# Sliding window attention with a normalized MLP: output buffers of group 0, column halves of W1, and the places of period 1's steps changed

## The chip, the cores and the metric

The kernel runs on one core of one Trainium2 chip. The metric is the time of one execution on the device, in microseconds (us). Engines: PE is TensorE, DVE is VectorE, ACT is ScalarE, POOL is GpSimd, SP is SyncE, which here only issues DMAs.

## The reference

For 8 batches of 576 positions and 8 heads of 64:

```python
scores = q @ k.T / 8              # per batch and head
mask = (rel >= 0) & (rel < 64)    # rel = query position - key position
attn = softmax(where(mask, scores, -1e9))
x = (attn @ v) with the heads side by side          # 8 x 576 x 512
xn = (x - mean) / sqrt(var + 1e-6) * g_ln           # over the 512 columns
out = x + relu(xn @ w_ch1) @ w_ch2                  # 512 -> 2048 -> 512
```

All inputs and the output are float32. The kernel casts what PE reads to float16 (f16) and accumulates in float32.

## The kernel before, in words

**Groups and periods.** Group g (0 to 7) is the first 512 positions of batch g; group 8 collects the last 64 positions of all eight batches, as four "tails" of two batches each. Period g is the loop turn in which the MLP of group g runs on PE. The attention of group g + 1 is worked in between, and the loads and casts of batch g + 2 go on beside it. Periods 6 and 7 carry the tails.

**A list of units and slots.** `mlp_units` returns the MLP of a group as a list of closures. The loop at the end of the kernel emits unit i, then every step that `at(i, ...)` put into slot i. The program order of each engine is that order; nothing is rescheduled later, and each engine works its queue strictly in order. `bz(i, g, j)` puts three steps of block j into slots i, i + 1 and i + 2: `b_step` (the product of the softmax weights with V, called the PV step, then on DVE the reciprocal, the scaling and the mean and variance: together a normalization), `r_step` (two ACT instructions for the reciprocal root) and `z_step` (DVE: the normalized block in f16). `zt_step` transposes z on PE into PSUM, and ACT copies it to zT, which the first product reads.

**First product.** `l1_half` (L440) makes two 128 x 256 results in one bank, `l1` (L408) one 128 x 512 result; either is 0.86 to 0.87 us of PE, and ACT applies relu (L445, L412). Group 0 has 8 half units and 8 whole ones, group 1 has 16 half units, the others 16 whole ones. They use the two banks of pool `ps_mm`.

**Second product.** Group 0 multiplies plainly: `l2_two` (L455) for output blocks 0 and 1, `l2` (L420) for blocks 2 and 3, and `add_out` (L429) adds x on DVE into a single buffer `osb1`, of which there are two, and appends a store on POOL's queue. All other groups use Strassen's scheme with seven products of half width (`product`, L480, units 16 to 29). `presum` makes the half sums on DVE (L398), `t_weights` those of the weights (L386, once). `post` (L495) adds a product into a pair buffer `osb`; a product that accumulates into a bank which an addition still reads has to wait for that addition. Bank X lives in pool `ps_t`, which has two banks, so that while X is held, transposes share the other bank.

**Attention.** `s_mm` computes the scores of one block of 128 queries against their keys (L279) into the two banks of pool `ps_s`, then ACT applies exp (L289, L283). The mask is either two matmuls ahead of the scores, which write a large negative bias (`pe_mask=True`, L261), or a product with 0 and 1 on DVE behind exp (`s_mask`, L296).

**Q, K and V.** SP loads them (L78, L83, L90, L144), POOL casts them (`cast_q` L131, `cast_v` L150). Batches below `NPE` are transposed on PE (`t_main`, L221, eight 128 x 128 transposes into PSUM and one copy on ACT or DVE, L213 or L215); the others by DMA from SP's queue (`x_main`, L233 and L239). `vB` is V shifted by 64 rows: for batches 0 and 1 copied by ACT and DVE (`vB_cur`, `vB_prev`), afterwards by two DMAs of POOL (`make_vB`, L168). `pace` (L348) is a one-column POOL copy that makes POOL wait for a certain result.

**Weights.** W1 is loaded in eight pieces of 256 rows x 512 columns; pieces 2q and 2q + 1 make the column quarter q. `w1_cast` scales by g and casts: chunk c = 0 of quarters 0 and 1 on POOL (L195), c = 1 on ACT (L193); quarters 2 and 3 on DVE and ACT. W2 is loaded in eight chunks into the same four staging buffers and cast on POOL (`w2_cast`, L205): chunk i serves unit `l2_two(i)`, and chunk i + 4 is loaded once chunk i has been cast.

**Warming matmuls.** `keep_clock` issues matmuls whose result nobody reads, at the start, while PE would otherwise idle.

Of the kernel before, what the change touches and what calls it, by code (L numbers as in the profile page):

```python
# [18 lines left out]
def kernel(  # L19
# [15 lines left out]
    NGRP = B + 1  # L35
    NPE = 4
    NKC = DM // 128
# [81 lines left out]
    def cast_qk(b, half):  # L119
        for x in range(2):  # L120
            cast_q(b, x, half)
# [130 lines left out]

    def s_mm(g, j, pe_mask=False):
        sc = [ps_s.tile([128, NHP, 2, 64], FP32, tag="sc", name=f"sc_{g}_{j}_{par}") for par in range(2)]
        pt = p_pt.tile([128, 2, NHP, 2, 64], FP16, tag="pt", name=f"pt_{g}_{j}")
# [144 lines left out]
    def mlp_units(g, split=0, two=False):  # L400
# [12 lines left out]

        ch = {}

# [11 lines left out]
        def add_out(kb):  # L427
            o = p_blk.tile([128, DM], FP32, tag="osb1", name=f"osb_{g}_{kb}", bufs=2)
            nc.vector.scalar_tensor_tensor(  # L429
                out=o, in0=ch[kb], scalar=rss[(g, kb)][:, 0:1],  # L430
                in1=x_norm[(g, kb // 2)][:, kb % 2].rearrange("p h d -> p (h d)"), op0=ALU.mult, op1=ALU.add,
            )
            stores.append((cur[0], nc.gpsimd, out[g, 128 * kb:128 * kb + 128, :], o))
# [28 lines left out]
        lo, hi = slice(0, 256), slice(256, 512)  # L462
        xyz, oo = {}, {}

# [80 lines left out]
    nc.vector.tensor_scalar(out=mbias, in0=mask, scalar1=-1.0, scalar2=30000.0, op0=ALU.add, op1=ALU.mult)  # L545
    for b in range(2):
        alloc_qkT(b)
        alloc_v(b)
        init_vB(b)
    cast_qk(0, 0)  # L550
    cast_v(0, 0, 1)
# [6 lines left out]
    w1_cast(1, 0, nc.gpsimd, 256, 512)  # L558
    w1_cast(2, 0, nc.gpsimd)
    w1_cast(3, 0, nc.gpsimd)  # L560

    warm = ps_mm.tile([128, 512], FP32, tag="mm", name="warm")

    def keep_clock(n):
# [24 lines left out]
    keep_clock(1)  # L589
    t_main(0, 1, 1, 0)  # L590
    keep_clock(2)
    b_step(0, 1)
    z_step(0, 1)
    keep_clock(2)
    vB_prev(0, 2, 0)
    vB_cur(0, 3, 1)
    s_mm(0, 2, True)
    zt_step(0, 0)
    w1_cast(0, 1, nc.scalar)
    b_step(0, 2)  # L600
    z_step(0, 2)
    zt_step(0, 1)
    w1_cast(1, 1, nc.scalar)
# [10 lines left out]
    def rest_of_loads():  # L614
        for i in range(8):
# [11 lines left out]
    TAILS = {  # L627
        6: ((0, load_tail, 0), (3, cast_tail, 0), (7, x_tail, 0), (14, s_mm, 8, 0), (15, s_mask, 8, 0),
            (20, b_step, 8, 0), (26, zt_step, 8, 0),
            (9, load_tail, 1), (12, cast_tail, 1), (16, x_tail, 1), (20, load_tail, 2), (24, cast_tail, 2),  # L630
            (28, x_tail, 2)),
        7: ((0, s_mm, 8, 1), (1, s_mask, 8, 1), (6, b_step, 8, 1), (12, zt_step, 8, 1),
            (6, s_mm, 8, 2), (7, s_mask, 8, 2), (11, b_step, 8, 2), (17, zt_step, 8, 2),
            (0, load_tail, 3), (3, cast_tail, 3), (7, x_tail, 3), (14, s_mm, 8, 3), (15, s_mask, 8, 3),
            (20, b_step, 8, 3), (26, zt_step, 8, 3)),
    }
    for g in range(NGRP):
# [12 lines left out]
        if g == 0:  # L650
# [5 lines left out]
            at(1, zt_step, 0, 2)  # L656
            at(3, zt_step, 0, 3)
            for j in range(4):
# [19 lines left out]
            at(29, vB_cur, 1, 3, 0)  # L678
            at(29, s_mm, 1, 2, True)
            at(30, s_mm, 1, 3, True)  # L680
            at(30, load_v, 2, 0, 4)
            bz(31, 1, 2)
            at(21, cast_q, 2, 0, 0)
            at(22, lambda: pace(zT[1][:, 0, 0:1]))
            at(22, cast_q, 2, 1, 0)
            at(27, cast_q, 2, 0, 1)
            at(29, lambda: pace(qkT[1][1][:, 0, 320:321]))
            at(29, cast_q, 2, 1, 1)
            for u, i, c in ((25, 1, 0), (25, 1, 1), (26, 2, 0), (28, 2, 1)):
                at(u, t_weights, i, c)  # L690
        if g == 1:
            at(0, alloc_qkT, 2)
            bz(1, 1, 3)
            at(2, zt_step, 1, 2)
            at(5, zt_step, 1, 3)
            at(4, alloc_v, 2)
# [4 lines left out]
            at(2, t_main, 2, 0, 0, 1)  # L701
            at(3, t_main, 2, 1, 0, 0)
            at(4, t_main, 2, 0, 1, 1)
            at(6, t_main, 2, 1, 1, 0)
            at(18, t_main, 3, 0, 0, 0)
            at(20, t_main, 3, 1, 0, 0)
            at(24, t_main, 3, 0, 1, 0)
            at(26, t_main, 3, 1, 1, 0)
            for j in range(4):
                at(8 + 4 * j, s_mm, 2, j)  # L710
                at(9 + 4 * j, s_mask, 2, j)
                bz(12 + 4 * j, 2, j)
                at((18, 22, 25, 28)[j], zt_step, 2, j)
        if g > 0:
            if g == 1:
                for u, i, c in ((5, 4, 0), (6, 4, 1), (7, 3, 0), (8, 3, 1)):
                    at(u, t_weights, i, c)
            for u, i, c in ((10, 3, 0), (12, 3, 1), (14, 1, 0), (14, 2, 0), (15, 4, 0), (16, 1, 1), (17, 2, 1), (18, 4, 1)) if g == 1 else (
                    (6, 3, 0), (10, 3, 1), (12, 1, 0), (13, 2, 0), (14, 4, 0), (16, 1, 1), (17, 2, 1), (18, 4, 1)):
                at(u, presum, g, i, c)  # L720
# [19 lines left out]
        if 0 < g and b + 1 < B:  # L740
# [68 lines left out]
```

## Time and profile before

| what | value |
|---|---|
| median of 9 runs | 327.81 us |
| lowest and highest run | 325.5 and 330.06 us |
| the profiled execution | 329.89 us |
| its span, first to last instruction | 328.2 us |
| PE busy | 305.2 us |
| DVE busy | 204.0 us |
| ACT busy | 173.4 us |
| POOL busy | 127.3 us |
| mean TensorE clock granted | 0.974 |

The profile is that of one execution, so its times are compared with the 329.89 us of that execution, which is 1.69 us more than its span. "Busy" is the time in which an engine works on an instruction; a PE that is busy at half clock counts as fully busy. In the views quoted below a name such as `hps<-zT,w1g` reads "writes hps, reads zT and w1g", L408 is a line of the kernel, and a bracket at the end of a line gives the idle time of the engine before it and what ended it.

### The profile page before, as it was taken

How to read it: one execution, taken by the hardware profiler on the slowest of the kernel's cores; microseconds unless marked ns; L12 is line 12 of the kernel's file. 1: busy time of each engine (PE TensorE's matmuls, PEld its weight loads, DVE VectorE, ACT ScalarE, POOL GpSimd, SP SyncE). 2: the span in 40 equal slices, each digit the busy share in tenths (PEclk: the TensorE clock that was granted, in tenths of full speed). 3: DMA queues.
4: the chain of work that ended last, by engine and by line, in shares of the span. 5: the costliest groups of instructions: out<-in, count | busy, mean ns of one | idle time of the engine just before them, and what ended most of it. 6: DMA issues, size and time to landing. Idle time of an engine off the chain costs nothing.

```text
span 328.2 us, 7591 instructions
## 1 busy us (share of the span) xinstructions
PE 305.2 (93%) x3097; PEld 201.6 (61%) x3097; DVE 204.0 (62%) x363; ACT 173.4 (53%) x347; POOL 127.3 (39%) x211
## 2 busy tenths in 40 slices
PE   6978998689959999999999999999999999899993
PEld 2446444368848646855784487458646864685582
DVE  0782568356777358827873785569459945862351
ACT  2597734248625686168427833863478157515600
POOL 6573747550812461355244425433445052101000
PEclk9999999959969999999999999999999999999998
DMA  8999999499840798699949895960696989203004
GB/s 180 265 391 267 362 289 274 125 281 268 214 99 0 170 214 175 143 259 168 218 96 270 137 241 99 267 132 11 149 238 141 159 182 189 52 2 128 0 2 128
DMA packets 119987, 57.30 MB, mean 175 GB/s; under 512 B 96080, under 2 KB 112976, under 8 KB 119952
## 3 DMA queue, kind: packets, MB, share of 16 engines
q1 hardware_dynamic: 115888, 45.10, 61.6%
q0 software_dynamic: 3104, 11.19, 11.1%
q10 hardware_dynamic: 960, 0.53, 0.6%
q8 instruction: 24, 0.39, 0.5%
q14 instruction: 11, 0.09, 0.1%
HBM read 38.80 MB, written 9.44 MB: 147 GB/s over the span
## 4 chain that ended last, share of the span: by engine, by line
PE 67%; DVE 8%; ACT 7%; DMA 5%; SPq 5%; POOL 3%; issue 3%; DVEq 0%; POOLq 0%
PE hps L408 24%; PE wX L480 16%; PE wZ L480 8%; PE hph L440 5%; PE wY L480 4%; PE xps L312 3%; PE sc L279 3%; DMA w1s<-in_moe_w_ch_dram 2%; SPq L144 2%; POOL w1g L195 2%; PE ztp L356 2%; PE tp L221 2%; ACT hrT L412 2%; DMA tv<-in_v_dram 2%; DVE stats L320 2%
## 5 line engine op out<-in xcount | busy, mean ns | idle before, releaser
L408 PE MATMUL hps<-zT,w1g 128*128 128x512 f16 x480 | 112.3, 379 | 0.9
L412 ACT ACTIVATE hrT<-hps 128x512 f16<-128x512 f32 x120 | 71.4, 597 | 31.3 <-PE hps L408 30.4
L408 PEld LDWEIGHTS <-w1g 128*128 128x128 f16 x480 | 44.9, 98 | 53.2 <-issue 5.9
L480 PEld LDWEIGHTS <-sw 128*128 128x128 f16 x512 | 49.6, 99 | 6.9 <-issue 0.6
L480 PEld LDWEIGHTS <-hrT 128*128 128x128 f16 x384 | 37.1, 99 | 6.2
L359 ACT COPY zT<-ztp 128x512 f16<-128x512 f16 x36 | 21.0, 583 | 35.4 <-PE ztp L356 35.3
L398 DVE TENSOR_TENSOR sw<-hrT 128x1024 f16<-128x1024 f16 x32 | 21.8, 680 | 20.6 <-ACT hrT L412 20.6
L440 PE MATMUL hph<-zT,w1g 128*128 128x256 f16 x192 | 25.8, 285 | 6.7 <-DVE osb L429 4.3
L131 POOL CAST qk<-qk 128x1024 f16<-128x1024 f32 x24 | 26.4, 1098 | 12.9 <-PE hph L440 5.0
L331 ACT ACTIVATE rs<-mv,epst 128x1 f32<-128x1 f32 x36 | 10.6, 296 | 37.5 <-DVE mv L322 37.3
L296 DVE TENSOR_TENSOR pt<-pt,mask 128x1024 f16<-128x1024 f16 x28 | 19.2, 687 | 14.4 <-ACT pt L283 7.4
L348 POOL CAST tok<-hrT 128x1 f32<-128x1 f16 x29 | 11.8, 408 | 41.1 <-ACT hrT L412 30.5
L289 ACT ACTIVATE pt<-sc 128x512 f16<-128x512 f32 x40 | 21.7, 594 | 9.0 <-PE sc L279 8.5
L315 DVE RECIPROCAL rcp<-xps 128x8 f32<-128x8 f32 x36 | 7.4, 204 | 30.0 <-PE xps L312 29.9
L320 DVE BATCH_NORM_STATS2 stats<-xn 128x6 f32<-128x512 f32 x36 | 25.0, 695 | 1.2
L318 DVE TENSOR_TENSOR xn<-xps,rcp 128x512 f32<-128x512 f32 x36 | 24.9, 691 | 1.2
L440 PEld LDWEIGHTS <-w1g 128*128 128x128 f16 x192 | 18.8, 102 | 11.1 <-issue 6.0
L495 DVE TENSOR_TENSOR osb<-wX,xn 128x512 f32<-128x512 f32 x24 | 16.4, 685 | 13.1 <-PE wX L480 13.1
L369 POOL DMA_DIRECT2D out_dram<-osb x18 | 12.6, 698 | 26.9 <-DVE osb L495 21.1
L150 POOL CAST vA<-v 128x512 f16<-128x512 f32 x32 | 21.4, 674 | 2.6 <-DMA v<-in_v_dram 2.6
L342 DVE TENSOR_SCALAR z<-xn,mv,rs 128x512 f16<-128x512 f32 x32 | 19.5, 611 | 0.8 <-ACT rs L332 0.6
L312 PEld LDWEIGHTS <-pt 128*64 128x64 f16 x576 | 12.5, 113 | 10.6 <-issue 7.4
(77 smaller groups left out, 453.1 us busy)
## 6 DMA issues: line engine op xcount, KB each, us to landing
qk<-in_q_dram SPq DMA_DIRECT2D x16, 512.0 KB, 5.9
v<-in_v_dram SPq DMA_DIRECT2D x32, 256.0 KB, 6.7
out_dram<-osb POOLq DMA_DIRECT2D x14, 512.0 KB, 7.2
w2s<-in_moe_w_ch_dram SPq DMA_DIRECT2D x12, 512.0 KB, 6.2
qk<-in_k_dram SPq DMA_DIRECT2D x8, 512.0 KB, 6.7
qk<-in_k_dram SPq DMA_DIRECT2D x16, 256.0 KB, 5.6
w1s<-in_moe_w_ch_dram SPq DMA_DIRECT2D x4, 512.0 KB, 7.0
tk<-in_k_dram SPq DMA_DIRECT2D x8, 256.0 KB, 5.0
```

Source lines behind the costliest of these rows:

```text
L131: nc.gpsimd.tensor_copy(out=dst[:, :].rearrange("p (a j) e d -> p a e j d", j=j), in_=t[:, :].rearrange("p (a e j d) -> p a e j d", e=2, j ...
L150: nc.gpsimd.tensor_copy(out=vA[b][:, c0:c1, :, 0:D], in_=v32[b][:, c0:c1])
L289: nc.scalar.activation(out=pt[:, par], in_=sc[par], func=AF.Exp, bias=0.0, scale=scale)
L312: nc.tensor.matmul(out=xps[64 * r:64 * r + 64, h, :D + 1], lhsT=pt[:, par, hp, r, :], rhs=rhs, start=True, stop=True)
L318: nc.vector.tensor_tensor(out=xn, in0=xps[:, :, 0:D], in1=rcp_b, op=ALU.mult)
L320: nc.vector.bn_stats(out=stats, in_=xn.rearrange("p h d -> p (h d)"))
L359: nc.scalar.copy(out=dst, in_=ztp)
L398: nc.vector.tensor_tensor(out=S[i], in0=a, in1=b, op=op)
L408: nc.tensor.matmul(out=hps, lhsT=w1g[:, kc, 128 * hc:128 * (hc + 1)], rhs=zT[g][:, kc, :], start=(kc == KCS[0]), stop=(kc == KCS[-1]),)
L412: nc.scalar.activation(out=hrT[:, hc, :], in_=hps, func=AF.Relu, bias=0.0, scale=1.0)
L440: nc.tensor.matmul(out=hps[:, e], lhsT=w1g[:, kc, 128 * hc:128 * (hc + 1)], rhs=zT[g][:, kc, 256 * half:256 * half + 256], start=(kc == KC ...
L480: nc.tensor.matmul(out=xyz[bank][:, t], lhsT=lhsT, rhs=rhs, start=bool(first and t == 0 and hc == 0), stop=(t == 1 and hc == 7), skip_grou ...
```

## The change

Batch 3 is transposed by DMA and no longer on PE (`NPE` is 3). Group 0's outputs go to two pair buffers, from the same pool tag as the other groups'. Quarter 1 of W1 is cast on POOL by column halves, both pieces' first halves ahead of the second ones. The masks of group 1 move from PE to DVE. In the prologue POOL's memsets are spread behind the first casts, V's shifted copies go ahead of the first scores, scores (0, 1) use the banks of `ps_mm`, the first PV step comes directly behind the first two scores, and there are fewer warming matmuls. In periods 1 and later the scores, normalizations and transposes of period 1 get other slots, the sums S4 (`presum` 4) go to slots 20 and 22, and tails 0 and 3 are attended later.

```diff
-    NPE = 4
+    NPE = 3
...
-    def s_mm(g, j, pe_mask=False):
-        sc = [ps_s.tile([128, NHP, 2, 64], FP32, tag="sc", name=f"sc_{g}_{j}_{par}") for par in range(2)]
+    def s_mm(g, j, pe_mask=False, pool=None):
+        pool, tag = (ps_s, "sc") if pool is None else pool
+        sc = [pool.tile([128, NHP, 2, 64], FP32, tag=tag, name=f"sc_{g}_{j}_{par}") for par in range(2)]
...
-        ch = {}
+        ch, oo = {}, {}
...
         def add_out(kb):
-            o = p_blk.tile([128, DM], FP32, tag="osb1", name=f"osb_{g}_{kb}", bufs=2)
+            if kb % 2 == 0:
+                oo[kb // 2] = p_blk.tile([128, 2, DM], FP32, tag="osb", name=f"osb_{g}_{kb}", bufs=2)
+            o = oo[kb // 2][:, kb % 2]
...
-    for b in range(2):
-        alloc_qkT(b)
-        alloc_v(b)
-        init_vB(b)
-    cast_qk(0, 0)
+    alloc_qkT(0)
+    cast_q(0, 0, 0)
+    alloc_v(0)
+    cast_q(0, 1, 0)
+    init_vB(0)
...
-    w1_cast(2, 0, nc.gpsimd)
-    w1_cast(3, 0, nc.gpsimd)
+    for lo in (0, 256):
+        for i in (2, 3):
+            w1_cast(i, 0, nc.gpsimd, lo, lo + 256)
+
+    for f in (alloc_qkT, alloc_v, init_vB):
+        f(1)
...
-    keep_clock(9)
-    t_main(0, 0, 0)
-    keep_clock(2)
-    t_main(0, 1, 0)
-    keep_clock(4)
+    keep_clock(9, ps_mm, "mm")
+    t_main(0, 0, 0, 0)
+    keep_clock(1, ps_mm, "mm")
+    t_main(0, 1, 0, 1)
+    keep_clock(1, ps_mm, "mm")
+    vB_cur(0, 0, 0)
+    vB_cur(0, 1, 0)
+    vB_prev(0, 0, 1)
+    vB_prev(0, 1, 1)
     s_mm(0, 0, True)
-    vB_cur(0, 0, 1)
-    vB_prev(0, 0, 1)
-    vB_cur(0, 1, 1)
-    vB_prev(0, 1, 1)
-    keep_clock(3)
-    s_mm(0, 1, True)
+    s_mm(0, 1, True, (ps_mm, "mm"))
     b_step(0, 0)
     z_step(0, 0)
-    keep_clock(2)
-    vB_cur(0, 2, 0)
     t_main(0, 0, 1, 0)
+    b_step(0, 1)
+    z_step(0, 1)
     keep_clock(1)
     t_main(0, 1, 1, 0)
+    zt_step(0, 0)
+    vB_cur(0, 2, 0)
     keep_clock(2)
...
         6: (... 
-            (14, s_mm, 8, 0), (15, s_mask, 8, 0), (20, b_step, 8, 0), (26, zt_step, 8, 0),
+            (20, s_mm, 8, 0), (21, s_mask, 8, 0), (26, b_step, 8, 0),
         7: (...
+            (2, zt_step, 8, 0),
-            (14, s_mm, 8, 3), (15, s_mask, 8, 3), (20, b_step, 8, 3), (26, zt_step, 8, 3)),
+            (16, s_mm, 8, 3), (17, s_mask, 8, 3), (22, b_step, 8, 3), (27, zt_step, 8, 3)),
...
-            at(3, zt_step, 0, 3)
+            at(2, zt_step, 0, 3)
...
-            at(16, s_mm, 1, 0, True)
-            at(17, s_mm, 1, 1, True)
-            bz(18, 1, 0)
+            at(16, s_mm, 1, 0)
+            at(17, s_mask, 1, 0)
+            at(17, s_mm, 1, 1)
+            at(18, s_mask, 1, 1)
+            bz(19, 1, 0)
...
-            at(29, s_mm, 1, 2, True)
-            at(30, s_mm, 1, 3, True)
+            at(29, s_mm, 1, 2)
+            at(30, s_mask, 1, 2)
+            at(30, s_mm, 1, 3)
+            at(31, s_mask, 1, 3)
...
+            at(20, alloc_qkT, 2)
...
-            at(29, lambda: pace(qkT[1][1][:, 0, 320:321]))
...
-            at(18, t_main, 3, 0, 0, 0)
-            at(20, t_main, 3, 1, 0, 0)
-            at(24, t_main, 3, 0, 1, 0)
-            at(26, t_main, 3, 1, 1, 0)
             for j in range(4):
-                at(8 + 4 * j, s_mm, 2, j)
-                at(9 + 4 * j, s_mask, 2, j)
-                bz(12 + 4 * j, 2, j)
-                at((18, 22, 25, 28)[j], zt_step, 2, j)
+                at((8, 12, 15, 19)[j], s_mm, 2, j)
+                at((9, 13, 16, 20)[j], s_mask, 2, j)
+                bz((12, 16, 19, 23)[j], 2, j)
+                at((19, 23, 25, 28)[j], zt_step, 2, j)
...
-            ... ((10, 3, 0), (12, 3, 1), (14, 1, 0), (14, 2, 0), (15, 4, 0), (16, 1, 1), (17, 2, 1), (18, 4, 1)) if g == 1 else (
-                    (6, 3, 0), (10, 3, 1), (12, 1, 0), (13, 2, 0), (14, 4, 0), (16, 1, 1), (17, 2, 1), (18, 4, 1)):
+            ... ((10, 3, 0), (12, 3, 1), (14, 1, 0), (15, 2, 0), (16, 1, 1), (17, 2, 1), (20, 4, 0), (22, 4, 1)) if g == 1 else (
+                    (6, 3, 0), (10, 3, 1), (13, 1, 0), (14, 2, 0), (16, 1, 1), (17, 2, 1), (20, 4, 0), (22, 4, 1)):
                 at(u, presum, g, i, c)
...
-            if n < NPE:
+            if g == 1:
                 at(10, alloc_qkT, n)
                 (the casts of batch 3 at 9, 11, 13 and 15, as before)
+                at(13, x_main, n, 0)
+                at(17, x_main, n, 1)
```

More of the change, by code (lines that the diff above doesn't have):

```diff
@@ L462, in mlp_units @@
         lo, hi = slice(0, 256), slice(256, 512)
-        xyz, oo = {}, {}
+        xyz = {}
         def product(n, t):
@@ L558, with keep_clock @@
     w1_cast(1, 0, nc.gpsimd, 256, 512)
-    w1_cast(2, 0, nc.gpsimd)
-    w1_cast(3, 0, nc.gpsimd)
-    warm = ps_mm.tile([128, 512], FP32, tag="mm", name="warm")
-    def keep_clock(n):
+    for lo in (0, 256):
[3 more added lines that the diff above has]
+        f(1)
+    def keep_clock(n, pool=ps_t, tag="tp"):
+        warm = pool.tile([128, 512], FP32, tag=tag, name="warm")
         m = mbias[:, :]
@@ L569, in keep_clock @@
                              start=True, stop=True)
-    keep_clock(9)
-    t_main(0, 0, 0)
-    keep_clock(2)
-    t_main(0, 1, 0)
-    keep_clock(4)
-    s_mm(0, 0, True)
-    vB_cur(0, 0, 1)
-    vB_prev(0, 0, 1)
-    vB_cur(0, 1, 1)
-    vB_prev(0, 1, 1)
-    keep_clock(3)
-    s_mm(0, 1, True)
+    keep_clock(9, ps_mm, "mm")
[7 more added lines that the diff above has]
+    vB_prev(0, 1, 1)
+    s_mm(0, 0, True)
+    s_mm(0, 1, True, (ps_mm, "mm"))
     b_step(0, 0)
     z_step(0, 0)
-    keep_clock(2)
-    vB_cur(0, 2, 0)
     t_main(0, 0, 1, 0)
+    b_step(0, 1)
+    z_step(0, 1)
     keep_clock(1)
     t_main(0, 1, 1, 0)
+    zt_step(0, 0)
+    vB_cur(0, 2, 0)
     keep_clock(2)
[L592 to L595, printed above, removed]
+    s_mm(0, 2, True)
     vB_cur(0, 3, 1)
-    s_mm(0, 2, True)
-    zt_step(0, 0)
+    keep_clock(1)
+    zt_step(0, 1)
     w1_cast(0, 1, nc.scalar)
@@ L601 @@
     z_step(0, 2)
-    zt_step(0, 1)
+    vB_prev(0, 2, 0)
     w1_cast(1, 1, nc.scalar)
@@ L627 @@
     TAILS = {
-        6: ((0, load_tail, 0), (3, cast_tail, 0), (7, x_tail, 0), (14, s_mm, 8, 0), (15, s_mask, 8, 0),
-            (20, b_step, 8, 0), (26, zt_step, 8, 0),
+        6: ((0, load_tail, 0), (3, cast_tail, 0), (7, x_tail, 0), (20, s_mm, 8, 0), (21, s_mask, 8, 0),
+            (26, b_step, 8, 0),
             (9, load_tail, 1), (12, cast_tail, 1), (16, x_tail, 1), (20, load_tail, 2), (24, cast_tail, 2),
             (28, x_tail, 2)),
-        7: ((0, s_mm, 8, 1), (1, s_mask, 8, 1), (6, b_step, 8, 1), (12, zt_step, 8, 1),
+        7: ((0, s_mm, 8, 1), (1, s_mask, 8, 1), (2, zt_step, 8, 0), (6, b_step, 8, 1), (12, zt_step, 8, 1),
             (6, s_mm, 8, 2), (7, s_mask, 8, 2), (11, b_step, 8, 2), (17, zt_step, 8, 2),
-            (0, load_tail, 3), (3, cast_tail, 3), (7, x_tail, 3), (14, s_mm, 8, 3), (15, s_mask, 8, 3),
-            (20, b_step, 8, 3), (26, zt_step, 8, 3)),
+            (0, load_tail, 3), (3, cast_tail, 3), (7, x_tail, 3), (16, s_mm, 8, 3), (17, s_mask, 8, 3),
+            (22, b_step, 8, 3), (27, zt_step, 8, 3)),
     }
@@ L691 @@
         if g == 1:
-            at(0, alloc_qkT, 2)
             bz(1, 1, 3)
@@ L695 @@
             at(5, zt_step, 1, 3)
+            at(2, t_main, 2, 0, 0, 1)
+            at(3, t_main, 2, 1, 0, 0)
+            at(4, t_main, 2, 0, 1, 1)
+            at(6, t_main, 2, 1, 1, 0)
             at(4, alloc_v, 2)
@@ L717 @@
                     at(u, t_weights, i, c)
-            for u, i, c in ((10, 3, 0), (12, 3, 1), (14, 1, 0), (14, 2, 0), (15, 4, 0), (16, 1, 1), (17, 2, 1), (18, 4, 1)) if g == 1 else (
-                    (6, 3, 0), (10, 3, 1), (12, 1, 0), (13, 2, 0), (14, 4, 0), (16, 1, 1), (17, 2, 1), (18, 4, 1)):
+            for u, i, c in ((10, 3, 0), (12, 3, 1), (14, 1, 0), (15, 2, 0), (16, 1, 1), (17, 2, 1), (20, 4, 0), (22, 4, 1)) if g == 1 else (
+                    (6, 3, 0), (10, 3, 1), (13, 1, 0), (14, 2, 0), (16, 1, 1), (17, 2, 1), (20, 4, 0), (22, 4, 1)):
                 at(u, presum, g, i, c)
```

4 lines of the change are left out of this document (removed).

## The prediction, made before the result was known

> **What bounds the kernel now.** I read the page's head first, then the waits of PE, then the stretches, then the chain of waits where PE stands.
>
> ```profile
> PE 305.2 (93%) x3097; PEld 201.6 (61%) x3097; DVE 204.0 (62%) x363; ACT 173.4 (53%) x347; POOL 127.3 (39%) x211
> PEclk9999999959969999999999999999999999999998
> ```
>
> PE is busy for 93% of the span, so the work itself is the bound nearly everywhere. The clock row shows the exceptions: slices 9 and 12 (8.2 us each, about 66 to 74 and 90 to 98 us) ran below full speed. Both lie in period 1. The waits of PE say what stood in front of them:
>
> ```profile
> PE hph L440 <- DVE osb L429: 4.3, 2, 2.6
> PE ztp L356 <- ACT qkT L213: 3.4, 1, 3.4
> ...
> PE sc L279 <- DMA tkT<-tk: 0.8, 1, 0.8
> PE wX L480 <- DVE osb L495: 0.6, 1, 0.6
> ```
>
> The columns are the total, the number of waits and the longest. Only these four concern the change. The stretches show what the first two cost beyond the waiting (PE busy is the second column, the clock the third from the end):
>
> ```profile
> 66.00:68.00 2.00, 1.17 (x6) 0.86 (x6) 1.27 (x3) 0.98 (x3) 0.92 (x4) 0.50 1.31 258
> ...
> 70.00:72.00 2.00, 2.00 (x17) 1.71 (x15) 1.13 (x3) 0.83 (x3) 1.23 (x2) 0.50 1.11 339
> ...
> 94.00:96.00 2.00, 1.98 (x12) 1.52 (x12) 1.93 (x4) 0.58 (x1) 0.65 (x2) 0.50 0.00 0
> ```
>
> After each wait PE works at half clock for some 5 us. The first wait in the chain:
>
> ```profile
> 59.79 2.53 DMA out_dram<-osb
> ...
> 62.41 0.76 DVE osb L429
> ...
> 66.05 0.74 DVE osb L429
> 66.83 1.87 PE hph L440 x8
> ```
>
> Group 0 has two single output buffers. The third addition waits until the first store has landed (62.32), although that store left POOL only at 59.79. The fourth comes a whole normalization later, at 66.05. PE needs both additions to free the two banks in which period 1 begins, so its second unit starts at 66.83, at half clock: 1.87 us for 8 matmuls.
>
> **The change part by part.** Unit prices first, from the chain and from DVE's timeline:
>
> ```profile
> 40.55 0.43 PE sc L261 x2
> ...
> 42.29 0.58 PE sc L261 x2
> ...
> 83.71 0.22 DVE rcp L315
> ...
> 85.41 0.18 DVE mv L322
> ...
> 86.77 1.18 DVE z L342
> ...
> 88.58 1.42 DVE sw L398
> ...
> 93.07 0.91 ACT qkT L213
> ...
> 104.17 0.37 PE xps L312 x16
> ...
> 105.52 0.22 PE ztp L356 x4
> 105.74 0.87 PE wZ L480 x8
> 106.62 0.45 PE tp L221 x8
> ...
> 109.91 0.86 PE hps L408 x4
> 110.77 0.34 PE sc L279 x16
> ```
> ```profile
> 92.99 0.68 DVE L495 TENSOR_TENSOR osb<-wX,xn 128x512 f32<-128x512 f32 x1
> 93.59 0.68 DVE L296 TENSOR_TENSOR pt<-pt,mask 128x1024 f16<-128x1024 f16 x1
> ```
> ```profile
> L342 DVE TENSOR_SCALAR z<-xn,mv,rs 128x512 f16<-128x512 f32 x32 | 19.5, 611 | 0.8 <-ACT rs L332 0.6
> ```
>
> A unit is 0.87 of PE, a normalization 1.8 of DVE (83.71 to the end of mv), and a mask follows an addition on DVE 0.6 after its start; I take the same for half sums.
>
> *To the second product half of group 0 (51.19 before).*
>
> ```profile
> L195 POOL TENSOR_SCALAR w1g<-w1s,g x5: 912/1557/1719, 18.3 to 23.4; 128x512 f16<-128x512 f32 x3, 128x256 f16<-128x256 f32 x2
> ```
> ```profile
> 25.01 1.81 PE L440 MATMUL hph<-zT,w1g 128*128 128x256 f16 x15 [1.19 <-POOL w1g L195]
> 27.98 3.85 PE L440 MATMUL hph<-zT,w1g 128*128 128x256 f16 x32 [0.94 <-ACT zT L359]
> ...
> 48.65 1.46 PE L455 MATMUL ch<-w2s,hrT 128*128 128x512 f16 x6
> ...
> 51.19 1.89 PE L420 MATMUL ch<-w2s,hrT 128*128 128x512 f16 x8
> ```
> ```profile
> 29.91 1.04 POOL L131 CAST qk<-qk 128x1024 f16<-128x1024 f32 x1 [4.96 <-PE hph L440]
> ...
> 46.65 1.04 POOL L205 CAST w2s<-w2s 128x1024 f16<-128x1024 f32 x1 [0.37 <-DMA w2s<-in_moe_w_ch_dram]
> ```
>
> A half cast is 0.91 us, a whole one 1.56 to 1.72. The third unit now needs two half casts fewer, so it can start 1.4 before 25.01; POOL ends its five casts' work 0.4 later. With block 3's transpose a slot earlier, the units at 27.98 start about 1.4 earlier; I carry 1.1 past the ScalarE casts that follow. Mask pairs of blocks 0 and 1 leave PE too (0.43 and 0.58). Unit l2_two(7), at 48.65, would then come at 46.5. But it reads W2's last chunk, which is cast from 46.65 to 47.7, when the DMA has brought it, and nothing in the change moves that DMA. Behind 47.7 come the unit (0.87), an addition (0.76), z (0.61) and the transposes: 50.2 in place of 51.19. **Minus 1.0**, bounds 0 (W1 gains nothing) and 1.3. The reordered prologue, with fewer warming matmuls, lies ahead of the same wait with 1.2 to spare; I cost it at nothing. Without that cover a half clock window would cost 1 to 2. Batch 1's memsets go behind W1's casts, into POOL's idle 4.96.
>
> *From there to the second unit of period 1 (66.83 before).* Mask matmuls of blocks 2 and 3 leave PE (1.0). PE ends group 0 at 59.5: 50.2, eight units, two transposes, two scores, one PV step, and 0.4 of waits for exponentials. The third addition, which waits for no store now, runs at 55.2. The fourth is still behind the moved masks (done at 59.2, behind exponentials) and block 2's normalization (61.0), and ends at 61.75. So PE's wait doesn't vanish: about 1.3 of 4.3 is left, on the same releaser. From 51.19 to 66.83 were 15.6; from 50.2 to 61.75 are 11.55. **Minus 4.1**, bounds 2.5 and 5.3 (no wait left). The pair buffers are next wanted by period 1's products, 20 us behind the stores.
>
> *To period 2's first PV step (rcp at 83.71 before).* From 66.83 PE has 12 units (10.45), four transposes (1.8), two of zT (0.44), two PV steps (0.74) and a score (0.34): 13.8, where 16.9 went. The half clock from 66.83 to 72 took 2.7 of that. With one wait of 1.3 left I expect no drop: **minus 3.1**, bounds 0.5 and 3.4. This PV step also needs the shifted copies of V:
>
> ```profile
> 72.03 0.53 POOL L168 DMA_DIRECT2D vB<-vA  x1 [0.30 <-POOL vA L150]
> ```
> ```profile
> DMA to landing us min/median/max: 5.0/6.8/8.3
> ```
>
> They left at 72.03, 11 us ahead of it. POOL's last store and casts now end earlier, and I get 68 for the copies and 75.5 for the step: 7.5 us for 5.0 to 8.3. I take no wait; the bound is 1.
>
> *To period 2's start (109.91 before).* That stretch is 26.2. Batch 3's four transposes leave PE (0.45 each) and ScalarE (0.91), and with them the wait of 3.4, where one stood behind a ScalarE copy that stood behind a normalization on DVE. What is late next is DVE. Up to the addition that frees the bank for the last product its queue holds four normalizations (7.2), seven half sums and three masks (6.0), three z (1.8), five additions (3.0): 18.0, and 1.3 for the two slow rows, 1.18 and 1.42. PE adds two units and a transpose (2.0): 21.3. PE's own work is 17.5 (17 units, two scores, three PV steps, four transposes of zT). So DVE decides; with 1.3 for waits inside its queue I take 22.6. **Minus 3.6**, bounds 2 (half clock comes back) and 8 (PE decides). The S4 sums' later place pays for the mask that moved ahead of the first addition.
>
> The Trainium skill, "SBUF — State Buffer", section "Who interferes with whom", says that a VectorE instruction with two SBUF inputs and a GpSimd instruction that reads SBUF shut each other out for a whole instruction. By that rule the four new masks of period 1 would each risk a POOL cast's length, and the sum would lose about 1 us more; the half sum of 1.42 agrees.
>
> Batch 3's six DMA transposes stand on SP's queue behind V's loads and ahead of batch 4's:
>
> ```profile
> 116.41 1.83 SPq L233 DMA_TRANSPOSE qkT<-qk  x1
> 118.36 2.50 SPq L239 DMA_TRANSPOSE qkT<-qk  x2
> ```
>
> Two such sets take 9 us of that queue with the gaps, from about 79 to 88, and period 2 opens at 98. Batch 4's loads wait behind them and are wanted after 100. Both are hidden, with some 7 us of cover.
>
> *Tails.* Tail 0 later removes the 0.6 in front of wX, tail 3 two units later the 0.8 in front of its scores. **Minus 1.0** (0 to 1.4), since both normalizations now lie nearer to the next start.
>
> **The sum.** 1.0 + 4.1 + 3.1 + 3.6 + 1.0 = 12.8. The profiled execution took 329.89 (span 328.2), so 317.1. It lies 2.08 above the median, 327.81. I put half of that down to the half clock stretches that go, so the median loses 11.8: **316.0 us**.
>
> **The rivals.**
>
> *The clock drops again in period 1 (20%).* PE would wait about 0.5 and 1.4 close together around the second products. For it: the drop before 66 came with waits of 1.7 and 2.6. Against it: waits of 1.19 and 0.94 before 28 us went by at full clock. A stretch of 5 us at half clock costs 2.5: 318.5. The Trainium skill, "TensorE: Matmul & The Clock Gate", section "Why this matters for your kernels", allows gaps up to about 3 us. By that rule there is no drop; the 2.6 here shows that less can do.
>
> *The wait moves instead of going (15%).* The fourth addition comes later still behind masks and normalization, and the V copies 1 to 2 us late. Then stretches two and three give 4.0 in place of 7.2: 319.2.
>
> *PE sets the pace in period 1 (10%).* DVE's queue drains faster than I add, and 18.5 does for the last stretch: 311.9.
>
> *SP's queue is late: slower (4%).* Period 2 opens with scores that read batch 3's transposes, and PE is in order. It decides only if they land after 111, 13.4 behind the 98 assumed: then all of the gain and 1.6 more are gone, 329.4 and up. The rows put them near 91.
>
> *The edits do nothing that PE feels (3%).* The additions wait on something other than the store: 327.8.
>
> **How the numbers follow.** The forecast has 48%. The range takes in the first three rivals and their bounds: 311 to 321. A measurement of this kernel can tell 0.5% (1.6 us). Faster by more: 0.93. Within: 0.03. Slower: 0.04.
>
> **What would show it.** Right: no addition waits for a store; full clock from 62 to 98; PE's wait on osb L429 near 1.3; l2_two(7) at the end of W2's last cast; DVE over 90% busy behind period 2's first PV step, with PE's waits on osb L495 at 2 or less; period 2 near 98; no wait for tkT. Wrong: the second unit of period 1 after 64, W2's last cast moved, period 2 after 102, or PE waiting for batch 3's transposes.

## The result, and the profile after

The kernel after took 320.57 us (median of 10 runs, 319.81 to 322.77) and the kernel before 327.75 (31 runs, 325.5 to 331.41). The ratio is 0.9787, with a 95% interval of 0.976 to 0.9814: faster by 7.2 us. The forecast was 316.0 (311 to 321), so sign and range held and the size was 4.6 too good. The profiled execution of the kernel after took 320.09 with a span of 318.4, so 9.8 less than the profiled execution of the kernel before. Runs that lie over 1.5% above the fastest run of the same kernel measured with them are left out of the ratios and of the table by clock below. The code is one to three lines further down now: `l1_half` is L443, `l1` L409, `l2_two` L458, `l2` L421, `add_out` L432, `post` L498, the mask on DVE L297.

The page's head, to be read beside the one of before:

```profile
PE 296.3 (93%) x3047; PEld 195.1 (61%) x3047; DVE 206.7 (65%) x365; ACT 171.0 (54%) x345; POOL 126.9 (40%) x212
PEclk9999999999999999999999999999999999999998
```

PE is 8.9 us less busy, with 50 matmuls fewer, and the clock row has no low slice. The stretches that ran at 0.50 before are at 1.00 (third figure from the end), although one of the two waits ahead of them is still there:

```profile
62.00:64.00 2.00, 0.43 (x4) 0.24 (x3) 1.93 (x4) 0.53 (x3) 0.00 (x0) 1.00 1.15 315
66.00:68.00 2.00, 2.00 (x25) 1.74 (x23) 1.93 (x4) 1.11 (x4) 1.76 (x4) 1.00 0.91 313
70.00:72.00 2.00, 2.00 (x26) 1.85 (x24) 1.53 (x2) 1.38 (x4) 0.00 (x0) 1.00 1.17 226
94.00:96.00 2.00, 1.74 (x16) 1.56 (x16) 2.00 (x4) 0.00 (x0) 1.13 (x3) 1.00 1.06 166
```

The waits of PE:

```profile
PE xps L313 <- DVE pt L297: 2.2, 2, 1.2
PE hph L443 <- DVE osb L432: 1.7, 1, 1.7
PE wX L483 <- DVE osb L498: 1.6, 3, 0.8
...
PE ch L458 <- POOL w2s L205: 0.9, 1, 0.9
```

The wait of 3.4 for a ScalarE copy of qkT and the wait for tkT are gone. The wait for group 0's additions fell from 4.3 to 1.7, and PE now waits for a mask on DVE. The places where the stretches end, and the rows that set them, on PE and then on DVE:

```profile
48.51 1.46 PE L458 MATMUL ch<-w2s,hrT 128*128 128x512 f16 x6 [0.87 <-POOL w2s L205]
...
50.75 1.89 PE L421 MATMUL ch<-w2s,hrT 128*128 128x512 f16 x8
...
64.09 1.03 PE L443 MATMUL hph<-zT,w1g 128*128 128x256 f16 x8 [1.66 <-DVE osb L432]
...
68.51 0.61 PE L221 MATMUL tp<-ident,qk 128*128 128x128 f16 x8 [0.49 <-ACT zT L360]
```
```profile
100.65 1.03 PE L409 MATMUL hps<-zT,w1g 128*128 128x512 f16 x4
```
```profile
55.63 0.73 DVE L432 SCALAR_TENSOR_TENSOR osb<-ch,rs,xn 128x512 f32<-128x512 f32 x1
...
58.16 3.46 DVE L297 TENSOR_TENSOR pt<-pt,mask 128x1024 f16<-128x1024 f16 x2
61.54 0.20 DVE L316 RECIPROCAL rcp<-xps 128x8 f32<-128x8 f32 x1
...
63.32 0.72 DVE L432 SCALAR_TENSOR_TENSOR osb<-ch,rs,xn 128x512 f32<-128x512 f32 x1
```
```profile
79.08 0.21 DVE L316 RECIPROCAL rcp<-xps 128x8 f32<-128x8 f32 x1 [1.54 <-PE xps L313]
```

From these rows and those of before:

| stretch | before ends | after ends | expected | measured |
|---|---|---|---|---|
| to the second product half of group 0 | 51.19 | 50.75 | −1.0 | −0.4 |
| to the second unit of period 1 | 66.83 | 64.09 | −4.1 | −2.3 |
| to period 2's first PV step | 83.71 | 79.08 | −3.1 | −1.9 |
| to period 2's first unit of `l1` | 109.74 | 100.65 | −3.6 | −4.5 |
| to the end of the span | 328.2 | 318.4 | −1.0 | −0.7 |
| sum | | | −12.8 | −9.8 |

### The profile page after: what moved, and what is told of

Read it like the earlier page. It is cut to its first block, busy times and chain, and to the rows that moved or that the text cites. A ratio compares the mean times of both kernels' runs of the same rounds, so it can differ in the third digit from the quotient of the medians.

```text
span 318.4 us, 7507 instructions
## 1 busy us (share of the span) xinstructions
PE 296.3 (93%) x3047; PEld 195.1 (61%) x3047; DVE 206.7 (65%) x365; ACT 171.0 (54%) x345; POOL 126.9 (40%) x212
## 4 chain that ended last, share of the span: by engine, by line
PE 63%; DVE 13%; ACT 5%; issue 1%
PE hps L409 27%; PE wX L483 15%; PE wZ L483 7%; PE wY L483 3%; PE hph L443 3%; PE xps L313 3%; PE sc L280 3%; DVE osb L498 2%; DVE sw L399 2%; ACT hrT L413 2%; DVE stats L321 2%; DVE xn L319 2%; DVE pt L297 2%; ACT pt L284 2%; DVE tw L387 1%
## 5 line engine op out<-in xcount | busy, mean ns | idle before, releaser
L409 PE MATMUL hps<-zT,w1g 128*128 128x512 f16 x480 | 112.3, 379 | 1.4 <-ACT zT L360 0.3
L409 PEld LDWEIGHTS <-w1g 128*128 128x128 f16 x480 | 45.0, 97 | 54.2 <-issue 6.9
L399 DVE TENSOR_TENSOR sw<-hrT 128x1024 f16<-128x1024 f16 x32 | 22.9, 715 | 25.1 <-ACT hrT L413 25.1
L297 DVE TENSOR_TENSOR pt<-pt,mask 128x1024 f16<-128x1024 f16 x32 | 24.7, 775 | 14.9 <-ACT pt L284 9.2
L131 POOL CAST qk<-qk 128x1024 f16<-128x1024 f32 x22 | 23.8, 1081 | 11.4 <-DMA qk<-in_q_dram 7.4
L443 PE MATMUL hph<-zT,w1g 128*128 128x256 f16 x192 | 24.3, 273 | 3.0 <-DVE osb L432 1.7
L498 DVE TENSOR_TENSOR osb<-wX,xn 128x512 f32<-128x512 f32 x24 | 16.5, 687 | 12.6 <-PE wX L483 12.6
L284 ACT ACTIVATE pt<-sc 128x512 f16<-128x512 f32 x40 | 21.7, 596 | 1.8
L443 PEld LDWEIGHTS <-w1g 128*128 128x128 f16 x192 | 17.9, 98 | 6.7 <-issue 2.3
L290 ACT ACTIVATE pt<-sc 128x512 f16<-128x512 f32 x32 | 17.2, 596 | 4.6 <-PE sc L280 4.2
```

What stands on the lines that cost most here:

```text
L131: nc.gpsimd.tensor_copy(out=dst[:, :].rearrange("p (a j) e d -> p a e j d", j=j), in_=t[:, :].rearrange("p (a e j d) -> p a e j d", e=2, j ...
L284: nc.scalar.activation(out=pt[:, par].rearrange("k h w (p j) -> k (h w) p j", j=4), in_=sc[par][:, :].rearrange("k h w (j p) -> k (h w) p ...
L297: nc.vector.tensor_tensor(out=ptv, in0=ptv, in1=mb, op=ALU.mult)
L399: nc.vector.tensor_tensor(out=S[i], in0=a, in1=b, op=op)
L409: nc.tensor.matmul(out=hps, lhsT=w1g[:, kc, 128 * hc:128 * (hc + 1)], rhs=zT[g][:, kc, :], start=(kc == KCS[0]), stop=(kc == KCS[-1]),)
L443: nc.tensor.matmul(out=hps[:, e], lhsT=w1g[:, kc, 128 * hc:128 * (hc + 1)], rhs=zT[g][:, kc, 256 * half:256 * half + 256], start=(kc == KC ...
```

## The experiments

**The kernel before once more.** The first question is whether the profiled execution of before, 2.1 above its median, was long for its low clock.

> The kernel before, once more, for its granted clock in several runs. Theory A (the profiled execution of before, 2 us above its median, had one half clock stretch more than most): most runs show a clock of 0.98 or more and the ones near 330 show 0.975 or less; this profile has one half clock stretch, not two. Rival B (both stretches are always there, the 2 us come from elsewhere): every run near 0.974, both stretches in the profile again.

It took 328.94, ratio 1.0023 (0.9977 to 1.007). Over 47 runs of the kernel before that were measured with the experiments, eight of these ten among them, time and mean clock go together:

| mean clock of the run | runs | times | median |
|---|---|---|---|
| 0.992 to 0.994 | 10 | 325.25 to 327.3 | 326.8 |
| 0.983 to 0.991 | 24 | 326.56 to 329.66 | 328.1 |
| 0.970 to 0.980 | 13 | 328.31 to 331.05 | 329.8 |

The profiled execution of before had 0.974 and belongs to the last row, whose median is 3.0 above that of the first. The kernel after ran at 0.985 to 0.999. So the profile of before shows more half clock than its median run had, and that part of the 9.8 is not in the median's 7.2. The other half of theory A, one half clock stretch in the new profile, did not come: that execution took 331.57 at 0.979, and it has both stretches. Which of the two a run near 0.99 lacks, no profile shows.

**The pair buffers alone**, put into the kernel before and nothing else:

```diff
-            o = p_blk.tile([128, DM], FP32, tag="osb1", ..., bufs=2)
+            if kb % 2 == 0:
+                oo[kb // 2] = p_blk.tile([128, 2, DM], FP32, tag="osb", ..., bufs=2)
+            o = oo[kb // 2][:, kb % 2]
```

> The kernel before with nothing but the two pair buffers for group 0's outputs. Theory (the wait for the store is the first large loss, and in the changed kernel the buffers gave back 4.1 us of it): PE's second unit of period 1 starts at 62 to 63 in place of 66.8, no half clock stretch before 74, total 4 to 6 us faster than before. Rival (the next thing in DVE's queue takes its place): the second unit at 65 or later and 0 to 2 us faster.

It took 323.75, ratio 0.9857 (0.9814 to 0.9899): 4.7 of the change's 7.2 from one edit. On PE:

```profile
63.52 1.03 PE L442 MATMUL hph<-zT,w1g 128*128 128x256 f16 x8 [0.77 <-DVE osb L431]
```
```profile
PEclk9999999999979999999999999999999999999998
```
```profile
PE ztp L356 <- ACT qkT L213: 3.4, 1, 3.4
...
PE sc L279 <- DMA tkT<-tk: 0.9, 1, 0.9
```

The low slice 9 went with the wait for the store; the other two waits stayed, and slice 12 is still below full. The masks are on PE here, yet the second unit starts at 63.52, earlier than the 64.09 of the whole change, although the second product half started later (51.54 for 50.75). That is the first sign that the moved masks cost something.

**The change without the pair buffers:**

```diff
-            if kb % 2 == 0:
-                oo[kb // 2] = p_blk.tile([128, 2, DM], FP32, tag="osb", ..., bufs=2)
-            o = oo[kb // 2][:, kb % 2]
+            o = p_blk.tile([128, DM], FP32, tag="osb1", ..., bufs=2)
```

> The changed kernel with the two single output buffers of group 0 back. Theory (the pair buffers took away the wait for the store): the third addition waits again for the first store to land, at 60 to 62, the fourth and PE's second unit of period 1 come at 66 or later, total 2 to 5 us slower than the changed kernel, more where the clock drops. Rival (the moved steps gave the gain): the same time as the changed kernel.

It took 324.71, ratio 0.991 (0.9878 to 0.9943): 4.1 above the change.

```profile
61.01 0.75 DVE L430 SCALAR_TENSOR_TENSOR osb<-ch,rs,xn 128x512 f32<-128x512 f32 x1 [4.69 <-DMA out_dram<-osb]
...
64.13 1.28 DVE L297 TENSOR_TENSOR pt<-pt,mask 128x1024 f16<-128x1024 f16 x2
...
67.37 0.75 DVE L430 SCALAR_TENSOR_TENSOR osb<-ch,rs,xn 128x512 f32<-128x512 f32 x1
```
```profile
PE xps L313 <- DVE pt L297: 6.3, 2, 5.3
```
```profile
67.13 3.62 PE L441 MATMUL hph<-zT,w1g 128*128 128x256 f16 x16
```

The third addition waits for the store again, 5.4 later than in the change, and everything on DVE queues behind it, the fourth addition too (67.37 in place of 63.32). PE waits 5.3 at once, and then needs 3.62 for 16 matmuls that take 1.9 at full clock. A side finding: two masks take 1.28 here. The last POOL cast ended at 63.65, ahead of them:

```profile
62.60 1.05 POOL L131 CAST qk<-qk 128x1024 f16<-128x1024 f32 x1
```

**The masks back on PE.** In the change the same two masks took 3.46. The rows of POOL beside them, and the first mask by itself:

```profile
58.49 1.05 POOL L131 CAST qk<-qk 128x1024 f16<-128x1024 f32 x1
...
60.01 1.05 POOL L131 CAST qk<-qk 128x1024 f16<-128x1024 f32 x1
```
```profile
58.16 1.93 DVE L297 TENSOR_TENSOR pt<-pt,mask 128x1024 f16<-128x1024 f16 x1
```

Each mask ends 0.55 behind a cast: 60.09 after 59.54, and 61.62 after 61.06. The first theory was that each waits for the cast beside it. The test puts group 1's masks back on PE:

```diff
-            at(29, s_mm, 1, 2)
-            at(30, s_mask, 1, 2)
-            at(30, s_mm, 1, 3)
-            at(31, s_mask, 1, 3)
+            at(29, s_mm, 1, 2, True)
+            at(30, s_mm, 1, 3, True)
```
(and the same for blocks 0 and 1 in slots 16 to 18.)

> The changed kernel with group 1's masks back on PE as mask matmuls. Theory (POOL's casts, which run beside them, stretch the two DVE masks of blocks 2 and 3 from 0.7 to 1.7 us each, so that moving them off PE lost there what it gained): the second unit of period 1 starts at 62.5 to 63.5 in place of 64.1, the rest is as in the changed kernel; total the same or 1 us faster. Rival (the masks' move was itself worth the 1.0 us of PE that it saves): the second unit at 65, 1 us slower.

It took 320.12, ratio 0.976 (0.9712 to 0.9807), not to be told from the change. Its profiled execution is one of the two fastest of its runs, 318.28, and there the second unit starts earlier:

```profile
62.46 0.82 PE L443 MATMUL hph<-zT,w1g 128*128 128x256 f16 x6 [0.77 <-DVE osb L432]
```

So the masks on DVE gained nothing in time: what PE was spared came back as a wait.

The change has a hand in where the casts lie. With the buffers alone batch 2's last two casts start on POOL at 61.77 and 63.41, in the change at 58.49 and 60.01, right beside the masks. Its diff drops the `pace` ahead of the last one; no run puts that line back by itself.

**The casts moved away from the masks.** The masks stay on DVE, and batch 2's last two casts wait on POOL until block 2's normalization is done:

```diff
-            at(27, cast_q, 2, 0, 1)
-            at(29, cast_q, 2, 1, 1)
+            at(32, lambda: pace(mvs[(1, 2)][:, 0:1]))
+            at(32, cast_q, 2, 0, 1)
+            at(32, cast_q, 2, 1, 1)
```

> The changed kernel with the last two casts of batch 2's Q and K moved on POOL from slots 27 and 29 to behind block 2's variance (slot 32). Theory (a POOL cast that reads SBUF shuts out a DVE instruction with two SBUF inputs): the two masks take 0.7 us each and not 1.7, the second unit of period 1 starts at 62.0 to 62.6, total 1.5 to 2 us faster than the changed kernel. Rival (the masks are slow by themselves there, or wait for exp): both still take 1.7, second unit at 64, total the same.

It took 318.21 (317.95 to 319.46), ratio 0.9725 (0.9677 to 0.9773). All of its six runs are below the lowest, 319.65, of the sixteen runs of the kernel after.

```profile
57.28 2.13 DVE L297 TENSOR_TENSOR pt<-pt,mask 128x1024 f16<-128x1024 f16 x2
```
```profile
61.91 1.03 PE L443 MATMUL hph<-zT,w1g 128*128 128x256 f16 x8 [0.77 <-DVE osb L432]
```

The two masks take 2.13 in place of 3.46 (one cast, at 57.19, still lies beside the first), and the second unit starts 2.2 earlier: 1.35 from the masks, and 0.83 because the second product half started at 49.92 in this execution. The median fell by 2.4. It is the lowest median of the versions tried, but the next two runs lie within its interval.

**Both at once:** masks on PE and casts late.

> The kernel after, with the masks of group 1 back on TensorE and batch 2's last two casts moved late as well. Theory (the masks cost only where a cast lies beside them; with the casts gone, a mask on VectorE takes 0.7 and is nearly free): putting the masks on TensorE gains nothing more, the second unit starts at 61.9 to 62.5, and the time is 318 to 320, not below the 318.2 of the casts alone. Rival (the masks on VectorE cost by their own length, casts or not): the two gains add, the second unit starts near 61.0 and the time is 316.5 to 317.5.

It took 319.33 (318.65 to 320.12), ratio 0.9728 (0.9684 to 0.9773): no gain over the casts alone. The second unit did not start at 61.9 to 62.5 as forecast:

```profile
63.92 1.03 PE L443 MATMUL hph<-zT,w1g 128*128 128x256 f16 x8 [0.77 <-DVE osb L432]
```

In this execution the second product half was late, at 51.94, because PE waited 1.93 for block 1's z on DVE. The time between the two tells more than the places:

| run | second product half | second unit | between |
|---|---|---|---|
| the change | 50.75 | 64.09 | 13.34 |
| the change, once more | 50.58 | 63.80 | 13.22 |
| whole casts of W1 | 50.99 | 64.12 | 13.13 |
| batch 3 on PE | 49.91 | 63.15 | 13.24 |
| buffers alone | 51.54 | 63.52 | 11.98 |
| masks on PE | 50.47 | 62.46 | 11.99 |
| casts later | 49.92 | 61.91 | 11.99 |
| both | 51.94 | 63.92 | 11.98 |

With the masks on PE, or the casts moved, or both, it is 12.0; with masks beside casts it is 13.1 to 13.3. So the theory held: a mask on DVE costs this stretch nothing once the casts are moved, and beside them the two cost 1.2 to 1.4. Nothing in this stretch tells the four runs with 12.0 apart.

**The fourth addition first.** What PE still waits for there is the addition, which stands behind block 2's normalization on DVE. Here it stands ahead of it:

```diff
-            bz(31, 1, 2)
+            bz(32, 1, 2)
...
-            at(27, cast_q, 2, 0, 1)
-            at(29, cast_q, 2, 1, 1)
+            at(32, lambda: pace(pts[(1, 3)][:, 0, 0, 0, 0:1]))
+            at(32, cast_q, 2, 0, 1)
+            at(32, cast_q, 2, 1, 1)
```

> The kernel after, with batch 2's last two casts moved behind the last mask of period 1, and the normalization step of block 2 issued one slot later, so that on VectorE the fourth addition stands ahead of it. In the run with the casts alone moved, the second unit's product started at 61.91 after waiting 0.77 for the addition. Theory (the addition's place in VectorE's queue is all that TensorE still waits for there): the second unit starts at 61.0 to 61.3, and the time is 0.7 to 1.0 below that run's 318.2, at 317.3 to 317.6. Rival (block 2's normalization is then late for its transposes at the start of period 2, or the later casts meet the masks of the next blocks): the second unit gains the same, but TensorE waits for the normalization by about as much, and the time is 318.2 or above.

It took 318.42, ratio 0.9713 (0.9659 to 0.9766): the rival's number. The profiled execution is the slowest of the six (321.85), with W2's last cast late by 0.9 us against the change, so only its order is read. Its two masks have no cast beside them and take 0.69 each.

```profile
62.02 1.92 PE L443 MATMUL hph<-zT,w1g 128*128 128x256 f16 x16
...
65.39 1.03 PE L443 MATMUL hph<-zT,w1g 128*128 128x256 f16 x8 [1.07 <-ACT hrT L448]
...
69.42 0.61 PE L221 MATMUL tp<-ident,qk 128*128 128x128 f16 x8 [1.10 <-ACT zT L360]
```

The two first units run without a gap, and then PE waits 1.07 for a relu on ACT and 1.10 for the transposed z of block 2, which is now late. The gain of 0.8 that was forecast is given back one step on.

**Whole casts of W1 in the change:**

```diff
-    for lo in (0, 256):
-        for i in (2, 3):
-            w1_cast(i, 0, nc.gpsimd, lo, lo + 256)
+    w1_cast(2, 0, nc.gpsimd)
+    w1_cast(3, 0, nc.gpsimd)
```

> The changed kernel with W1's quarter 1 cast in whole pieces on POOL again. Theory (whatever is won at W1 is lost at W2's last chunk, which the DMA brings at the same time): the third unit starts 1 us later, the second half of group 0 within 0.3 us of the changed kernel's 50.75, total the same. Rival (the halves carry through): 1 us slower.

It took 320.41, ratio 0.9769 (0.9714 to 0.9824): no difference in time. The first `l1` unit of group 0 starts at 31.91 in place of 30.97, but the second product half at 50.99 in place of 50.75. The theory's result held, its reason only in part: in this execution W2's last cast came early, at 46.44, and another wait set the start of the second half:

```profile
50.76 0.40 PE L357 MATMUL ztp<-ident,z 128*128 128x128 f16 x4 [1.24 <-DVE z L343]
```

Block 1's normalization on DVE is the second bound there, close behind the first; in the run with both edits it was the one that decided.

**The old order of the first 30 us in the change** (before's block from `alloc_qkT` to the fourth scores, with W1's halves kept):

> The kernel after with the order of its first 30 us taken from the kernel before (the casts of W1's quarter 1 still by column halves). Theory (whatever the beginning gains is lost in the wait for W2's last cast, which sets the second product half of group 0): the second product half starts at 50.7 to 51.2 as in both kernels, and the time is 320 to 321, within 0.5 of the kernel after. Rival (the beginning carries some of the gain on its own): the second product half starts at 51.5 or later and the time is 321.5 to 323.

It took 322.79 (four runs), ratio 0.9826 (0.9769 to 0.9883), beside 320.83 for the change measured with it; the intervals overlap. Both theories were half right. The second product half started at 51.16, as the first said; the time was the rival's. The loss came later, at the masks:

```profile
58.69 3.91 DVE L297 TENSOR_TENSOR pt<-pt,mask 128x1024 f16<-128x1024 f16 x1
```
```profile
59.48 1.05 POOL L131 CAST qk<-qk 128x1024 f16<-128x1024 f32 x1
...
60.99 1.05 POOL L131 CAST qk<-qk 128x1024 f16<-128x1024 f32 x1
```
```profile
64.00:66.00 2.00, 2.00 (x9) 1.06 (x8) 1.93 (x5) 0.50 (x2) 0.00 (x0) 0.50 1.10 329
```

The first mask ends 0.56 behind the second cast here, PE waits 3.3 for it, and the clock falls to 0.50. The old beginning is not shown to be the cause: the run with the old tails has the new beginning, its first mask and its casts lie to each other as in the change, and the same happens there.

**Batch 3 back on PE** (`NPE` 4, its transposes in their old slots, its DMA transposes gone):

```diff
-    NPE = 3
+    NPE = 4
...
+            at(18, t_main, 3, 0, 0, 0)
+            at(20, t_main, 3, 1, 0, 0)
+            at(24, t_main, 3, 0, 1, 0)
+            at(26, t_main, 3, 1, 1, 0)
```

> The changed kernel with batch 3 transposed on PE again, in the old slots. Theory (period 1's second half is bound by DVE at 21.7 us, so PE's 1.8 us of transposes partly fit into its waits, but the ScalarE copies behind the reciprocal roots make PE wait again): the wait of a zT transpose for a ScalarE copy comes back with 1 to 3 us, period 2 starts 2 to 3.5 us later, total 2 to 3.5 us slower than the changed kernel. Rival (the wait went because the steps were moved apart): 0 to 1 us slower.

It took 321.75, ratio 0.9809 (0.9762 to 0.9856), 1.2 above the change, within the intervals. The wait for the ScalarE copy is back, in part:

```profile
PE ztp L357 <- ACT qkT L213: 1.9, 2, 1.7
```

From period 2's first PV step to period 2's start it takes 22.9 (78.13 to 101.02) where the change takes 21.6: 1.3 more, between the theory's 2 to 3.5 and the rival's 0 to 1.

**The old places of the tails in the change:**

> The changed kernel with the steps of tails 0 and 3 in their old slots. Theory (they removed two waits of 0.6 and 0.8 us in periods 6 and 7): both waits are back, total 0.7 to 1.4 us slower than the changed kernel. Rival (the tails' loads now come early enough by themselves): the same time, no wait.

It took 321.71 (317.95 to 323.54), ratio 0.9758 (0.9701 to 0.9814): the runs scatter too much to tell it from the change. In the profile the waits are back, and from period 2's first unit to the end it takes 219.4, where ten profiled executions with the new tails take 217.5 to 218.4 and the three of kernels with the old ones 218.5 to 219.1:

```profile
PE wX L483 <- DVE osb L498: 2.4, 4, 0.8
...
PE sc L280 <- DMA tkT<-tk: 1.3, 1, 1.3
```

The profiled execution, 323.54, is the longest of its six, 3.5 above that of the change. Of this 1.8 lies ahead of period 2: W2's last cast came at 48.30, and the first mask, which here too ends behind both casts (59.23 and 60.75), ended at 62.36:

```profile
58.90 4.06 DVE L297 TENSOR_TENSOR pt<-pt,mask 128x1024 f16<-128x1024 f16 x2
```

**The change itself, beside the last kernels.**

> The kernel after itself, so that the other kernels of this call have it beside them on the same chip. All theories: 320 to 321, ratio 0.976 to 0.981 to the kernel before, the two masks of blocks 2 and 3 at 3.3 to 3.6 together.

It took 320.83, ratio 0.9774 (0.9722 to 0.9826), and its two masks 3.5.

## Why the prediction was right in sign and 4.6 us off in size

The direction, the range and most of the mechanism held, but two of the signs named for being wrong came true as well: the second unit of period 1 came after 64, at 64.09, and W2's last cast moved. Period 2 opened at 100.65, between the 98 forecast and the 102 named as wrong. No wait of PE for batch 3's transposes came.

**The first stretch (−1.0 expected, −0.4 measured).** The step that failed is the time of W2's last cast, 46.65, taken as fixed. In the profiled execution of after it came 0.76 later, behind its DMA:

```profile
47.41 1.04 POOL L205 CAST w2s<-w2s 128x1024 f16<-128x1024 f32 x1 [1.80 <-DMA w2s<-in_moe_w_ch_dram]
```

The chain behind it was as forecast: cast, unit, addition, z, transposes. But the cast's time is no property of the change. In the nine profiled executions with the new beginning, W1's halves included, it starts anywhere from 46.5 to 48.3; the kernel before has 46.65 and, profiled again, 47.26. I took one execution's value for a constant, where it is spread by nearly 2 us. That W1's halves bring nothing in time was right; the run with whole casts adds a second bound, block 1's z.

**The second stretch (−4.1, −2.3).** The third addition did come free of the store (55.63; 55.2 expected), and that is the largest part of the gain, as the two runs with and without the buffers show (4.7 and 4.1). The step that failed is the price of the masks: at 0.6 each they were to be done at 59.2, where the two took 3.46 and were done at 61.62. The second unit came 2.3 later than the 61.75 forecast; 0.55 of that is the first stretch (50.75 for 50.2), and 1.8 this. The Trainium skill, "SBUF — State Buffer", section "Who interferes with whom", was cited for just this: a VectorE instruction with two SBUF inputs and a GpSimd instruction that reads SBUF exclude each other. The forecast gave it a sentence and no term. The runs agree with the rule: 1.28 for two masks with no cast beside them, 2.13 with one, 3.46 to 4.51 with two. The profile before has the other direction: POOL's casts at 86.15 and 87.93 each begin 0.06 to 0.07 behind a DVE instruction with two SBUF inputs and take 1.51 and 1.52 in place of 1.04. Moving the casts gained 2.4 us in the median; 1.35 of it is seen at the masks, and the rest, a second half that began 0.83 earlier in the profiled execution, lies ahead of the moved casts and isn't explained by them. Against the buffers alone, which take 11.98 for this stretch, the change's 13.34 is a loss: here the other edits cost 1.4. The rival "the wait moves instead of going" gave 4.0 for the second and third stretch in place of 7.2; they gave 4.2. Its condition, the fourth addition late behind masks and normalization, came true, by a dearer mask. Its other half did not: V's shifted copies left at 68.06, as forecast.

**The third stretch (−3.1, −1.9).** The clock did stay up, but the sum by unit prices, 13.8 of PE's work, was too short. The two stretches side by side (PE busy is the second column), after and before:

```profile
64.09:79.08 14.99, 14.50 (x192) 12.41 (x193) 8.73 (x15) 11.26 (x21) 6.79 (x14) 1.00 1.04 229
```
```profile
66.83:83.71 16.88, 16.88 (x192) 13.99 (x193) 8.81 (x14) 11.13 (x21) 7.17 (x15) 0.84 1.15 271
```

The same 192 matmuls take 14.50 at full clock. So 0.7 of the shortfall is my adding up, and 0.49 is the wait for zT at 68.51. The half clock had cost 2.4, not 2.7. The buffers alone bring this gain too: there the stretch takes 15.09.

**The fourth stretch (−3.6, −4.5).** Right, and a little better. DVE decides, as forecast: it is busy nearly without a gap from 79.08 to 99.8, and PE waits on osb 1.6 in all (2 or less expected). The 1.3 that I had added for waits inside its queue was nearly all unneeded. That batch 3's DMAs are hidden was right too: PE waits for no DMA transpose anywhere in the list. The same batch on PE puts 1.3 back, and with the buffers alone the stretch takes 25.1 in place of 26.0. What is left of the 4.5, about 2, goes with the new places of period 1's steps; no run has the old places back by themselves, so that share is argued and not shown. The rival in which PE sets the pace did not come about: DVE is busy 20.25 of the 20.72 us from 79.08 to 99.8.

**The tails (−1.0, −0.7).** Right in the profile; the total can't tell it.

**From the profile to the median.** I gave half of 2.08 to the half clock. The difference of the two profiles is 9.8 and that of the medians 7.2, so 2.6 lies there: 2.1 because before's profiled execution was one of the low-clock runs, 0.5 because after's is below its own median. So of the 4.6 that were missing, 3.0 are the stretches and 1.6 this step.

**The rival of a clock that drops again** did not come about in the profiled execution: with waits of 1.16 and 1.66 the clock stayed at 1.00. It came in the profiles with the old beginning and with the old tails, where PE waited 3.3 and 2.5 at once for a mask.

## What to carry to other kernels

When work with two SBUF inputs is moved to VectorE, lay the rows of GpSimd over the place it moves to, and price each instruction from its start to the end of the cast beside it, not by its median: here 0.65 became 1.7. Moving the GpSimd work a few slots back gave 2.4 us in the median, 1.35 of it seen at the masks. And if the profiled execution has a lower clock than most runs, the gain that it promises is too large: here all of the 2.1 that it lay above the median had to come off, not half.

## What the runs showed of the hardware that I had not expected

A masked product on DVE beside a POOL cast ends 0.55 behind the cast. When a second cast follows within 0.5, the mask sometimes gets in between (60.09, between casts at 58.49 and 60.01) and sometimes waits for both (58.69 to 62.60, behind casts at 59.48 and 60.99). In four executions it got in between, in two (those with the old beginning and the old tails) it waited for both, and the old tails have the same rows of mask and casts against each other as the change, to 0.01. In all six the mask's row begins ahead of the cast's, by 0.33 or more, so the order of the rows does not tell which holds the other. What decides stayed open.

The granted clock is a matter of degree over a few microseconds: waits of 1.16 and 1.66, some three microseconds apart, left it at 1.00; waits of 1.7 and 2.6 around one unit, or a single one of 3.3, 3.4 or 5.3, sent PE to half speed for about 3 to 7 us. Near the edge it goes both ways: a single wait of 2.15 (old tails, at 49.39) left it at 1.00, one of 2.24 at nearly the same place (addition first, at 49.41) sent it to 0.50, and so did one of 2.5 (old tails, at 62.41). Three microseconds of time between the runs of one and the same kernel go with it.

The arrival of one load, W2's last chunk, varies by nearly 2 us between executions: 46.5 to 48.3 for the cast, which waits for the load in seven of the nine executions with the same beginning. In these seven the row of its issue on SP's queue ends at 40.8 to 41.7, so most of the spread is the load's own. Two of the three longest of the nine, 321.85 and 323.54, had the cast at 48.3.
